# The order of VectorE, ScalarE, GpSimd and the transfers: from the framework's scheduler to a list schedule written in the kernel

## The chip, the cores and the metric

The kernel runs on one core of one Trainium2 chip. A core has five engines with a queue of instructions each: TensorE (PE, matmuls; PEld are its weight loads), VectorE (DVE), ScalarE (ACT), GpSimd (POOL) and SyncE (SP), which here only issues transfers. The metric is the device time of one execution in microseconds (us), the median of several runs. One more execution is taken with a profiler; its "span" runs from the first to the last instruction.

## The reference

A block over x of 2048 tokens by 512 features, all in float32. The weights are scaled so that sums are large, and the kernel computes each product of two float32 matrices from halves in float16.

```python
xn = layernorm(x)
# A: sliding-window attention, 32 heads of 16, window 256
q, k, v = split(xn @ wqkv)
p = softmax(where(mask, q @ k.T * 16**-0.5, -1e9))
s = (p @ v) @ wo
# B: gated feed-forward, 512 -> 1792 -> 512
h = silu(xn @ w1) * (xn @ w3)
g = silu(h @ w2)
out = x + s * g
```

## The kernel before

**Tiling.** The tokens go in NT = 4 passes t of 512; within a pass the attention goes by NG = 4 groups of 8 heads and two halves p, so there are 32 attention "units" (t, g, p). The feed-forward goes by 14 blocks f of 128 columns of w1, w3 and rows of w2. Every float32 operand is split into a high float16 part and the rest, and a product is three matmuls (high x high, high x low, low x high).

**A unit.** `pass1` (L588 to L606) forms scores for the row maxima: four times a matmul into a PSUM bank pair `s` or `po`, then a masked maximum on DVE (L600, accumulated into M). The maxima are scaled (L605, L606), turned by a small matmul (L615), copied (L621) and sent through DRAM into two extra rows of the query tile `qa` (L623, L625). Two units later `pass2` forms the scores the other way round with the maxima subtracted (L662), adds the mask on DVE (L669), takes the exponent on ACT (L672) and multiplies by the values (L690). `finish` copies the sums out of PSUM (ACT L700, DVE L703) and sends them on; `normalise` inverts the denominators (L727), has them spread by DMA, multiplies on POOL and splits the result (ACT L740, POOL L300).

**Dense work.** `project` makes queries and keys (PE L534, ACT L543, DVE L547, then to DRAM and back), `value` the values (PE L504, ACT L507). `gate_up` makes one block f (PE L856, 24 matmuls): a tanh on ACT (L867), two products on DVE (L871, L876), a split on ACT and POOL (L880, L300). `down` multiplies by w2 and accumulates over four groups of blocks (PE L901; ACT L914 or DVE L917). `total` multiplies by wo and forms the output (PE L943; DVE L938, L947).

**Weights.** In pass 0 every block of w1, w3, w2 is loaded as float32, its squares are summed (ACT L231 and L814, or DVE L233) to choose a power of two as its scale, and it is scaled and split (ACT L303, L304, POOL L300); the split halves are stored to DRAM and loaded back in passes 1 to 3. So pass 0 has much more ACT, POOL and transfer work than the others. The layernorm of pass t + 2 is prepared in pass t (L406 to L424: statistics, an inverse square root by Newton steps on tiles of 128 x 4, centring), and then turned by matmuls (L462, L471, L472).

**Memory.** Two PSUM banks `m` take turns for the dense products, two bank pairs `s` and one pair `po` serve the attention. 39 slots in SBUF (`fpool`) are handed out by hand (`take`, `give`) for weights and intermediate results.

**What sets the order.** The program is traced by a planner of its own (`spread`, `run`, `later`, `more`), which interleaves pieces of dense work between batches of attention. TensorE runs in exactly the order traced:

```python
ORDERED = {ENGINE.PE}
with _tile.TileContext(nc) as tc, tc.manual_schedule(engines=ORDERED):
    tile_block(tc, *args)
```

The four other queues are ordered by the framework's scheduler, which starts from the order traced; `urgent()` moves an instruction forward by a priority of 200. In the first part of the program eight ties by hand (`tc.issue_after`, with the dictionary `lasts` of instructions) put chosen instructions behind others on their engine. Semaphores follow from the data and the final order.

## Time and profile before

| | |
|---|---|
| median of 3 runs | 840.1 us (838.94 to 843.25) |
| profiled execution, span | 835.6 us |
| the median beside that span | 4.5 us longer |
| PE busy | 809.6 us, 97% |
| DVE, ACT, POOL busy | 614.4, 408.2, 196.7 us |
| HBM traffic over the span | 125 GB/s |

Matmuls overlap in the records, so that a full row of matmuls reads as busy throughout, and PE's idle time is the time in which none was under way. A wait in a row of the timeline stands in brackets behind the instruction that waited: how long its engine had been idle, and whose end let it go. Idle time of the four other engines costs nothing unless PE, or the end, waits for them.

### The profile page before, as it was taken

To read this page: it belongs to the slowest core of one execution; us is meant where nothing else is said; L and a number is where in the kernel's file an instruction comes from. 1 tells how busy PE (TensorE), PEld (TensorE's weight loads), DVE (VectorE), ACT (ScalarE), POOL (GpSimd) and SP (SyncE) were. 2 spreads that over 40 slices of the span, in tenths; PEclk is the share of its full clock that TensorE was granted. 3 is DMA by queue.
4 is the path that set the end of the run, shared out by engine and by line. 5 is a ranking of instruction groups with operands and counts; after the bars stand their busy time and mean duration, and the time that the engine had idled before them with its cause. 6 is when DMAs were issued, how large, how long until landed. Compare 5 with 4: busy or idle time off the path is not lost.

```text
span 835.6 us, 22584 instructions
## 1 busy us (share of the span) xinstructions
PE 809.6 (97%) x8750; PEld 381.5 (46%) x8750; DVE 614.4 (74%) x2034; ACT 408.2 (49%) x598; POOL 196.7 (24%) x325
## 2 busy tenths in 40 slices
PE   9999898899999999999999999999999999999998
PEld 4434344434444444444445444444444444444444
DVE  8788767966797767798778876687777777676435
ACT  6799776373436444344433444443444443443521
POOL 2236264051313203111110211121111104031211
PEclk9999999999999999999999999999999999999999
DMA  9977556146633453453442535533443443434101
GB/s 281 260 232 237 165 181 184 47 152 199 189 96 95 110 140 108 138 155 110 130 121 72 140 94 154 142 111 102 119 143 88 112 117 107 116 96 125 55 21 52
DMA packets 95323, 110.62 MB, mean 132 GB/s; under 512 B 17200, under 2 KB 60528, under 8 KB 95216
## 3 DMA queue, kind: packets, MB, share of 16 engines
q1 hardware_dynamic: 94928, 108.67, 44.9%
q8 instruction: 68, 1.11, 0.6%
q10 hardware_dynamic: 288, 0.52, 0.2%
q14 instruction: 39, 0.32, 0.1%
HBM read 76.28 MB, written 28.57 MB: 125 GB/s over the span
## 4 chain that ended last, share of the span: by engine, by line
PE 68%; DVE 9%; issue 7%; DMA 6%; ACT 5%; POOL 3%; SPq 2%; POOLq 0%; ACTq 0%; DVEq 0%
PE m L856 24%; PE m L901 13%; PE po L690 8%; PE m L534 6%; PE s L662 5%; PE m L943 4%; PE m L504 3%; POOL slot L300 3%; DVE junk L600 2%; PE s L588 2%; DMA slot<-in_B_w_dram 2%; DMA qa<-dQ 1%; DVE s L669 1%; PE po L588 1%; ACT slot L303 1%
## 5 line engine op out<-in xcount | busy, mean ns | idle before, releaser
L300 POOL TENSOR_TENSOR slot<-slot,slot 128x256 f16<-128x256 f32 (+1 forms) x228 | 148.3, 677 | 575.7 <-ACT slot L880 464.5
L856 PE MATMUL m<-XH,slot 128*128 128x512 f16 x896 | 267.3, 380 | 4.3 <-DVE slot L547 2.5
L672 ACT ACTIVATE pt<-s,es 128x1024 f32<-128x1024 f32 x152 | 167.7, 1113 | 180.5 <-DVE s L669 177.3
L856 PEld LDWEIGHTS <-slot 128*128 128x128 f16 x1344 | 124.8, 98 | 159.9 <-issue 17.7
L856 PE MATMUL m<-XL,slot 128*128 128x512 f16 x448 | 169.8, 379 | 0.0
L901 PE MATMUL m<-slot,slot 128*128 128x512 f16 x672 | 158.1, 383 | 2.2 <-DVE slot L917 1.0
L669 DVE TENSOR_TENSOR s<-s,MK 128x256 f32<-128x256 f32 (+2 forms) x280 | 118.6, 435 | 49.2 <-PE s L662 48.2
L600 DVE CUSTOM_DVE_ANT_0 junk<-s,MW 128x320 bf16<-128x320 f32 x276 | 134.3, 486 | 24.7 <-PE s L588 15.7
L901 PEld LDWEIGHTS <-slot 128*128 128x128 f16 x672 | 62.5, 98 | 82.2 <-issue 12.3
L600 DVE CUSTOM_DVE_ANT_0 junk<-po,MW 128x320 bf16<-128x320 f32 x172 | 83.7, 487 | 5.6 <-DVE al L272 0.4
L690 PE MATMUL po<-pt,V 64*32 64x320 f32 (+4 forms) x2880 | 77.7, 343 | 0.5 <-DVE pp L277 0.5
L880 ACT CAST slot<-slot 128x512 f16<-128x512 f32 x56 | 34.5, 616 | 67.4 <-DVE slot L876 67.1
L690 PEld LDWEIGHTS po<-pt,V 64*32 64x32 f32 x2880 | 51.9, 106 | 24.1 <-PE s L588 4.7
L662 PE MATMUL s<-qa,KA 50*64 50x320 f16 (+3 forms) x1472 | 58.0, 259 | 1.4 <-DVE M L600 0.6
L871 DVE SCALAR_TENSOR_TENSOR slot<-slot,m 128x512 f32<-128x512 f32 x56 | 38.3, 684 | 28.0 <-ACT slot L867 27.0
L662 PEld LDWEIGHTS <-KA 50*64 50x64 f16 x1472 | 30.2, 105 | 55.7 <-issue 36.1
L867 ACT ACTIVATE slot<-m,sgs 128x512 f32<-128x512 f32 x56 | 38.4, 685 | 27.8 <-PE m L856 27.6
L588 PE MATMUL s<-KA,qa 48*64 48x320 f16 (+2 forms) x648 | 45.3, 294 | 6.7 <-DVE M L600 4.0
L917 DVE SCALAR_TENSOR_TENSOR slot<-m,dsc,slot 128x512 f32<-128x512 f32 x48 | 35.9, 747 | 15.9 <-PE m L901 15.6
L876 DVE SCALAR_TENSOR_TENSOR slot<-m,slot 128x512 f32<-128x512 f32 x56 | 38.5, 688 | 12.3 <-PE m L856 11.4
L534 PE MATMUL m<-XH,whi 128*128 128x512 f16 x120 | 44.7, 381 | 1.4 <-DVE slot L876 0.9
L534 PE MATMUL m<-XL,whi 128*128 128x512 f16 x120 | 44.5, 379 | 0.0
(152 smaller groups left out, 870.7 us busy)
## 6 DMA issues: line engine op xcount, KB each, us to landing
slot<-dW SPq DMA_DIRECT2D x126, 256.0 KB
slot<-in_B_w_dram SPq DMA_DIRECT2D x42, 256.0 KB
dW<-slot SPq DMA_DIRECT2D x42, 256.0 KB
slot<-in_A_x_dram SPq DMA_DIRECT2D x30, 256.0 KB
KA<-dK SPq DMA_DIRECT2D x24, 288.0 KB
qa<-dQ SPq DMA_DIRECT2D x32, 192.0 KB
dQ<-slot SPq DMA_DIRECT2D x16, 256.0 KB
dK<-slot SPq DMA_DIRECT2D x16, 256.0 KB
```

The costliest lines, as they stand in the source:

```text
L300: op(out[:, c], a[:, c], b[:, c])
L534: nc.tensor.matmul(cell["pp"], a[:, k, c, :], b[:, c, :], start=(c, i) == parts[0][0], stop=(c, i) == parts[-1][-1])
L588: nc.tensor.matmul(s[64 * c:64 * c + 64, r, :n], qa[rows, 2 * p + a, ii * P + 64 * c:ii * P + 64 * c + 64], ka[rows, 2 * p + a, e - n:e], ...
L600: nc.vector.tensor_tensor_reduce(out=junk[:, :n], in0=s[:, r, :n], in1=mask, scale=1.0, scalar=NEG, op0=ALU.add, op1=ALU.max, accum_out=M[ ...
L662: nc.tensor.matmul(s[64 * h:64 * h + 64, r, o:o + 64 * n], ka[rows, 2 * p + a, 64 * (m + 4):64 * (m + 5)], qa[rows, 2 * p + a, 64 * (m + k ...
L669: nc.vector.tensor_add(v, v, MK[:, kind, of:of + n, :].unsqueeze(1).to_broadcast([P, 2 * len(which), n, 64]))
L672: nc.scalar.activation(pt, s, AF.Exp, scale=es)
L690: nc.tensor.matmul(cell["po"][32 * i:32 * i + 32, h, 64 * (m + k):64 * (m + k + n)], V[64 * h:64 * h + 64, (4 * t + m // 2) % VB, hd * VW: ...
L856: nc.tensor.matmul(cell[k], w[:, (a * NC + c) * P:(a * NC + c + 1) * P], b[:, c, :], start=c == 0 and i == 0, stop=c == NC - 1 and i == 2)
L867: nc.scalar.activation(sg, cell[0], AF.Tanh, scale=sg_scale[:, f:f + 1])
L876: nc.vector.scalar_tensor_tensor(sg, cell[1], 0.5 * HS / (WS * XS)**2, sg, op0=ALU.mult, op1=ALU.mult)
L901: nc.tensor.matmul(ps, hh[:, a * TW + b * P:a * TW + (b + 1) * P], w[:, c * D:(c + 1) * D], start=f == f0 and i == 0, stop=f == f1 - 1 and ...
```

## The change

The eight ties, the dictionary `lasts` and its assignments go. A function `listed(tc)` is called once the whole program has been traced. It works on the list of all instructions, before the framework schedules them:

- `arrange` finds which instruction depends on which, by the regions that they read and write, by the reuse of tiles and by their PSUM banks. It gives every instruction a price: for PE by columns, type and tile size, plus 160 ns where the tile size changes; for ACT 130 + 0.98 n, for DVE 80 + 1.05 n, for POOL 40 + 2.6 n ns, n being the elements per partition; 420 ns for the issue of a transfer, with a latency and a time by its bytes.
- `deadlines` takes PE's order with PE never waiting ("nominal") and goes back from it: the latest start of each other instruction that keeps PE in time.
- `listed` then simulates all five queues. PE goes in its own order. Each other engine takes, of what is ready, the instruction with the earliest deadline; it stays idle for a while if something more urgent is about to be ready. An instruction counts as ready somewhat later than its inputs are (up to 1 us, 4 us behind a transfer) where its deadline leaves 2 us. Transfers with a distant deadline stand back while over 1.5 us of transfers are under way. After the first, each of three rounds uses the round before to see what is coming; the shortest is kept.
- The order found is fixed: every instruction of DVE, ACT, POOL and SP is chained to the one before it on its queue. No semaphore belongs to such a link.

What PE does and in which order, the tiles, slots and transfers stay as they are.

```diff
     def split(hi, lo, raw, s):
-        lasts["hi"] = nc.scalar.activation(hi, raw, AF.Copy, scale=s)
-        lasts["cut"] = nc.vector.scalar_tensor_tensor(lo, raw, s, hi, op0=ALU.mult, op1=ALU.subtract)
+        nc.scalar.activation(hi, raw, AF.Copy, scale=s)
+        nc.vector.scalar_tensor_tensor(lo, raw, s, hi, op0=ALU.mult, op1=ALU.subtract)
...
-    with tc.issue_after(lasts["centre"].ins):
-        qk[0][3]((1,))
+    qk[0][3]((1,))
...
-    with tc.issue_after(lasts["hi"].ins), tc.issue_after(lasts["x"].ins):
-        qk[1][1]()
+    qk[1][1]()
...
+def arrange(tc):
...
+    def cost(i):
+        n = 1
+        for s, c in i.outs[0].ap[1:]:
+            n *= c
+        if i.engine == ENGINE.PE:
+            t = i.tile_size
+            return n * (4 if i.ins[0].dtype == F32 else 1) / 2.4 * t[0] * t[1] / P**2 + 2
+        kind = type(i).__name__
+        if kind == "InstDMACopy":
+            return 420
...
+        if i.engine == ENGINE.Activation:
+            return 130 + 0.98 * n + 50 * (len(i.outs) > 1)
+        if i.engine == ENGINE.DVE:
+            return 80 + 1.05 * n + (6 * n if kind == "InstReciprocal" else 0) + 45 * (len(i.outs) > 1)
+        return 40 + 2.6 * n
...
+    extra = [1350 + carry(i) if d else 130 if i.engine != ENGINE.PE else 180 for i, d in zip(made, dma)]
...
+            if i.engine != ENGINE.PE:
+                latest[k] = min([latest[a] - (extra[k] if made[a].engine != i.engine or dma[k] else 0)
+                                 for a in after[k]] + [end]) - took[k]
...
+def listed(tc):
...
+            if k is None:
+                can = sorted((k for k in waiting[e] if ready[k] <= s), key=lambda k: latest[k])
+                k = can[0]
+                if ready_then:
...
+                    for k in can:
+                        if all(latest[j] >= latest[k] or ready_then[j] >= s + took[k] or latest[j] + SLACK >= s + took[k]
+                               for j in coming):
+                            break
+                    else:
+                        t = min(j_t for j_t in (ready_then[j] for j in coming))
+                        free[e] = max(t, s + 1)
+                        continue
+                if dma[k] and pipe > s + BACK and latest[k] > s + NEAR:
+                    free[e] = min([pipe - BACK] + [ready[j] for j in waiting[e] if ready[j] > s])
+                    continue
...
+            for a in after[k]:
+                wanted[a] -= 1
+                when = done + (60 if dma[k] else extra[k] if made[a].engine != e else 0)
+                margin = AFTER_DMA if dma[k] else AFTER if made[a].engine != e else 0
+                ready[a] = max(ready[a], when, min(when + margin, latest[a] - CLOSE))
...
+        if best_end is None or max(start) < best_end:
+            best_end, best_order = max(start), order
+    for e in engines[1:]:
+        for a, b in zip(best_order[e], best_order[e][1:]):
+            tc.add_manual_dep(made[b], made[a].name,
+                              mybir.DependencyInfo(mybir.DependencyClass.NoSync, mybir.DependencyReason.DATA), reason="order")
...
+ROUNDS, SHIFT = 3, False
+SLACK, BACK, NEAR = 300, 1500, 5000
+AFTER_DMA, AFTER, CLOSE = 4000, 1000, 2000
...
     with _tile.TileContext(nc) as tc, tc.manual_schedule(engines=ORDERED):
         tile_block(tc, *args)
+        listed(tc)
```

## The prediction

> **What bounds the kernel now.** I read the page first, then stages, then what TensorE waits for, then the timeline around single waits. The page's busy times:

> ```profile
> span 835.6 us, 22584 instructions
> PE 809.6 (97%) x8750; PEld 381.5 (46%) x8750; DVE 614.4 (74%) x2034; ACT 408.2 (49%) x598; POOL 196.7 (24%) x325
> ```

> TensorE (PE) sets the time, and the change leaves its order and its work alone. So only its idle time can be won: 835.6 - 809.6 = 26.0 us. The table of stages (start:end, length, then busy time of PE, PEld, DVE, ACT, POOL; granted clock; DMA share; GB/s) says where that lies:

> ```profile
> 0.00:40.00 40.00, 37.41 (x198) 16.73 (x199) 30.68 (x116) 29.56 (x58) 10.42 (x41) 1.00 1.00 266
> 40.00:120.00 80.00, 72.61 (x649) 32.58 (x648) 64.00 (x257) 67.66 (x133) 35.82 (x56) 0.98 0.64 207
> 120.00:240.00 120.00, 110.84 (x1336) 54.37 (x1339) 90.05 (x343) 62.28 (x99) 40.21 (x63) 1.00 0.50 152
> 240.00:800.00 560.00, 557.02 (x6391) 262.68 (x6391) 413.52 (x1295) 242.50 (x299) 105.01 (x158) 1.00 0.40 114
> 800.00:836.00 36.00, 31.74 (x201) 15.12 (x180) 16.18 (x26) 6.22 (x10) 5.26 (x8) 1.00 0.14 42
> ```

> PE's idle time is 2.59 us to 40 us, 7.39 us from 40 to 120, 9.16 us from 120 to 240, only 2.98 us in the 560 us that follow, and 4.26 us at the end (0.4 of it past the span). 40 to 240 us is the stretch that holds 16.55 us, and there no other engine is full: DVE 154 of 200 us, ACT 130. The engines have the time; the question is in what order they spend it. The longest waits of PE by name:

> ```profile
> PE s L588 <- DVE M L600: 4.0, 2, 2.9
> PE m L856 <- DVE slot L547: 2.5, 3, 1.3
> PE po L588 <- DVE XL L472: 1.9, 2, 1.1
> ```

> All three end with a DVE instruction that frees a PSUM bank or fills an operand. The costliest single one, at 88 us, with an undisturbed run of 12 equal matmuls (501.49) for comparison:

> ```profile
> 88.38 0.41 PE L662 MATMUL s<-qa,KA 50*64 50x320 f16 x10
> 91.71 0.25 PE L588 MATMUL s<-KA,qa 48*64 48x128 f16 x4 [2.92 <-DVE M L600]
> 91.89 4.45 PE L901 MATMUL m<-slot,slot 128*128 128x512 f16 x12
> ...
> 501.49 2.76 PE L901 MATMUL m<-slot,slot 128*128 128x512 f16 x12
> ```

> PE stands 2.92 us, and then 12 matmuls take 4.45 instead of 2.76 us: 1.69 us more, the only stage with a granted clock under 1.00. What DVE did meanwhile, with one row of POOL:

> ```profile
> 83.89 0.69 DVE L414 TENSOR_SCALAR r<-ve 128x4 int32<-128x4 int32 x1
> ...
> 86.70 0.16 DVE L418 TENSOR_TENSOR sq<-r 128x4 f32<-128x4 f32 x1
> 86.77 2.55 POOL L300 TENSOR_TENSOR slot<-slot,slot 128x256 f16<-128x256 f32 x4 [0.33 <-POOL slot L300]
> ...
> 88.12 0.59 DVE L418 TENSOR_TENSOR sq<-r 128x4 f32<-128x4 f32 x1
> ...
> 89.57 0.17 DVE L421 TENSOR_SCALAR rs<-r 128x4 f32<-128x4 f32 x1
> ...
> 90.30 0.48 DVE L600 CUSTOM_DVE_ANT_0 junk<-s,MW 128x320 bf16<-128x320 f32 x1
> ```

> It worked on the layernorm of the next 512 tokens (rstd, L411 to L421), wanted much later, while the maxima that PE's bank waits for (L600) stood behind. The same instruction, L418, takes 0.16 us where POOL pauses (0.33 us up to 86.77) and 0.59 us while POOL runs. Two more, with another pattern: DVE idle behind ACT, which does other things first.

> ```profile
> 120.15 0.61 ACT L304 CAST slot<-slot 128x512 f16<-128x512 f32 x1
> 120.66 0.69 ACT L867 ACTIVATE slot<-m,sgs 128x512 f32<-128x512 f32 x1
> ...
> 121.38 0.69 DVE L871 SCALAR_TENSOR_TENSOR slot<-slot,m 128x512 f32<-128x512 f32 x1 [2.72 <-ACT slot L867]
> ...
> 143.72 0.63 ACT L814 ACTIVATE sqa<-slot 128x512 bf16<-128x512 f32 x1
> 144.25 0.19 ACT L814 ACTIVATION_READ_ACCUMULATOR sqa<-slot 128x1 f32 x1
> 144.34 0.57 ACT L700 COPY os<-po 128x512 f32<-128x512 f32 x1
> ...
> 144.94 0.62 DVE L703 TENSOR_TENSOR os<-os,po 128x448 f32<-128x448 f32 x1 [2.48 <-ACT os L700]
> ```

> Weight splits (L304) and weight squares (L814) are done ahead of a tanh (L867) and a copy (L700) for which DVE, and behind DVE PE, wait. Over the span the table of waits has these pairs, and SP's own longest:

> ```profile
> DVE slot L871 <- ACT slot L867: 27.0, 24, 2.7
> DVE os L703 <- ACT os L700: 27.5, 23, 4.6
> SPq L709 <- DVE os L703: 108.1, 28, 14.3
> ```

> So the stalls I looked at are of order, not of work. That is what the change touches.

> **The change, part by part.** No instruction is added or removed on any engine, and no transfer; what changes is the order on DVE, ACT, POOL and SP, and all of it is fixed in advance by a plan made with prices (`cost`) and PE's order.

> *The hand ties* (eight, all before the second attention unit, so in the first stage). They kept weight squares behind splits and projections. Their loss is covered if the plan puts the splits by their deadline, as it is made to. If not, a split waits for a pair of squares:

> ```profile
> L231 ACT ACTIVATE sqa<-slot 128x512 bf16<-128x512 f32 x34 | 21.3, 627 | 1.8 <-DMA slot<-in_A_wqkv_dram 1.3
> L231 ACT ACTIVATION_READ_ACCUMULATOR sqa<-slot 128x1 f32 x34 | 6.4, 189 | 0.0
> ```

> 2 x (0.63 + 0.19) = 1.6 us. Gain at most the 2.59 us of that stage less 1.05 us before the first matmul: 1.5 us. I take 0, keeping -1.5 to +1.6.

> *DVE, ACT and POOL from 40 to 240 us.* At stake are 16.55 us of idle time and 1.69 us of slow clock, 18.24 us. An order by PE's deadlines puts L600 before the rstd chain, L867 before L304, L700 before L814. Bounds: nothing recovered, or all. I take three quarters, 13.7 us, since the three stalls above are all of the kind that the deadline decides, and a plan with fixed prices will miss some. POOL has 76 of 200 us of work here and feeds weights that are needed later; its order has slack.

> *The same from 240 to 800 us.* 2.98 us can be won; I take half, 1.5 us. Here is also the largest risk: an order that stands almost without stalls is replaced. What it may cost depends on the plan's prices, and one of them is far off. It prices a matmul of L690 at n x 4 / 2.4 x 64 x 32 / 16384 + 2 ns:

> ```profile
> L690 PE MATMUL po<-pt,V 64*32 64x320 f32 x1024 | 48.7, 431 | 0.5 <-DVE pp L277 0.5
> L690 PE MATMUL po<-pt,V 64*32 64x192 f32 x512 | 21.8, 323 | 0.0
> L690 PE MATMUL po<-pt,V 64*32 64x128 f32 x448 | 19.9, 274 | 0.0
> L690 PE MATMUL po<-pt,V 64*32 64x64 f32 x512 | 16.7, 217 | 0.0
> L690 PE MATMUL po<-pt,V 64*32 64x256 f32 x384 | 15.9, 388 | 0.0
> L690 PE MATMUL po<-pt,V 64*32 64x320 f32 (+4 forms) x2880 | 77.7, 343 | 0.5 <-DVE pp L277 0.5
> ```

> That is 68.7, 42.0, 28.7, 15.3 and 55.3 ns for these forms, 133.7 us in all against 77.7 us measured; over 32 attention units 4.18 against 2.43 us each. The plan believes PE 1.75 us later behind each of these bursts than it is. A bank that is drained 1.75 us late costs PE nothing as long as the other bank lasts: 2.76 us for 12 matmuls, less the draining instruction:

> ```profile
> L876 DVE SCALAR_TENSOR_TENSOR slot<-m,slot 128x512 f32<-128x512 f32 x56 | 38.5, 688 | 12.3 <-PE m L856 11.4
> L419 DVE SCALAR_TENSOR_TENSOR sq<-sq,ve 128x4 f32<-128x4 f32 x12 | 3.7, 309 | 0.4
> ```

> 2.76 - 0.69 = 2.07 us, just above 1.75. So I take a loss of 2 us over the stretch; bounds 0 and 1.75 us for each of its 24 bursts (2344 of the 2880 matmuls are counted there, at 96 a unit), 42 us.

> *SP's queue.* All transfers but two of the first loads are issued by SP, and they are reordered too, past waits like L709's, of up to 14.3 us. Weights of the later passes are asked for two blocks of F ahead (24 + 12 matmuls each at 2.76 us a dozen, so over 16 us ahead), which covers one such wait; without that cover the longest would be a stall of 14.3 us. I take 0; the DMA share of 0.40 leaves room.

> *The end.* Stage five is PE's own work and the last sum and store; 0.

> Sum, on the profiled execution: 835.6 - 13.7 - 1.5 + 2.0 = 822.4 us of span. The median of the runs, 840.1 us, is 4.5 us above that span; 822.4 + 4.5 = 826.9. Forecast **827 us**, its own range 819 to 835.

> [...]

> **The rivals.**

> *A, all order.* The plan removes every stall and costs nothing: 835.6 - 18.24 - 2.98 - 1.5 + 4.5 = 817 us. For it: idle engines in every stage. Against: prices are fixed and durations aren't.

> *B, the early stalls come back elsewhere.* The plan prices an instruction like L419 at 80 + 1.05 x 4 = 84 ns; the row above has 309 on average. The twelve from L414 (83.89) to the end of L421 (89.74) took 5.9 us where the plan counts 12 x 84 ns, 1.0 us. A plan that thinks it fits the chain in before L600 is ready makes the very stall of 88 us again. ACT is also 85% busy from 40 to 120 us. A quarter is then recovered, 4.6 us, against the 2 us lost: 835.6 - 4.6 + 2.0 + 4.5 = 837.5 us, no change that a measurement can tell. Against: the plan works in single instructions, so L600 can step in between two of the chain. [...]

> *C, slower: the plan's late TensorE.* At each burst of L690, DVE takes something else in the 1.75 us by which the plan thinks PE late, and the drain comes after the other bank has run out. It decides from the point where DVE already stands over 0.3 us behind (2.07 - 1.75). Half of the 1.75 us lost at 24 bursts is 21 us; with half of the early gain, 9.1 us: 835.6 - 9.1 + 21 + 4.5 = 852 us. For it: DVE is 74% busy there (413.5 of 560 us), and the stretch has almost nothing to win. Against: the error is the same everywhere and deadlines decide by comparison; nine bursts that lose all 1.75 us (15.7 us) only cancel the gain.

> *D, the plan does nothing.* If its edges gave the order that was there, the time would be 840. The stalls shown are against its rule, so I give it little and count it with B.

> **How the numbers follow.** Forecast 0.53, A 0.11, B with D 0.17, C 0.19. 0.5% (4.2 us), about what a measurement of this kernel can tell, puts the borders at 835.9 and 844.3 us. Faster: forecast, A and a small part of B, 0.67. Same: the rest of B, 0.14. Slower: C, 0.19. The range runs from 815 us, below A, to 848 us, where the milder half of C is in; it leaves out the heavier C and little below A.

> **What would show it.** Right: PE's idle time from 40 to 240 us falls from 16.55 to about 5 us; no stage has a clock under 1.00; L871's wait for L867 and L703's for L700 shrink; L600 stands among the rstd chain; 240 to 800 us stays within some 4 us of idle. B: another wait of 2 us or more on L600 behind L411 to L421. C: waits of PE on DVE (L871, L876, L917) right behind L690 bursts, and idle time spread evenly over 240 to 800 us. Wrong altogether: a stall on a weight load or on a KA or qa transfer, that is, SP's queue.

## The result and the profile after

The changed kernel takes 832.8 us (median of 5 runs, 832.03 to 833.4), the kernel before 838.9 us beside it (median of 5, 837.18 to 843.25): a ratio of 0.9923, with a 95% interval of 0.99 to 0.9947. That is 5.8 us above the forecast of 827, inside its range and its likeliest case's own range, and faster by more than 0.5%. The gain, though, is 6.1 us where 13.1 (840.1 to 827) were forecast. Lines behind the removed `lasts = {}` carry numbers one lower in this kernel: L599 here is L600 before, L870 is L871, L702 is L703, and the rstd chain is L410 to L420.

The profile after, its head and busy times:

```profile
span 830.5 us, 22573 instructions
PE 808.1 (97%) x8750; PEld 381.9 (46%) x8750; DVE 636.6 (77%) x2034; ACT 409.2 (49%) x598; POOL 200.5 (24%) x325
```

Its table of stages, in the columns of the prediction:

```profile
0.00:40.00 40.00, 35.81 (x200) 16.79 (x201) 32.41 (x120) 29.68 (x57) 9.04 (x39) 1.00 1.01 278
40.00:120.00 80.00, 74.36 (x665) 33.53 (x664) 66.49 (x259) 66.77 (x129) 35.56 (x54) 0.96 0.67 194
120.00:240.00 120.00, 114.25 (x1390) 56.31 (x1388) 102.31 (x350) 66.45 (x105) 43.42 (x66) 0.99 0.53 159
240.00:800.00 560.00, 557.05 (x6369) 262.54 (x6368) 420.53 (x1283) 240.62 (x300) 107.14 (x160) 1.00 0.40 113
800.00:836.00 36.00, 26.60 (x134) 12.70 (x132) 14.90 (x24) 5.65 (x9) 5.32 (x8) 0.96 0.13 42
```

PE's idle time by stage went from 2.59 to 4.19 us, 7.39 to 5.64, 9.16 to 5.75, 2.98 to 2.95, and stayed at 3.9 at the end: 26.0 to 22.4 us in all. What grew is the time at half clock. The granted clock of 0.96 in the second stage and 0.99 in the third comes from two stretches of 6.83 and 3.41 us at half speed, 10.24 us together; before there was one of 3.41. The two now, in the same columns:

```profile
109.89:116.72 6.83, 5.49 (x17) 2.05 (x18) 6.45 (x29) 2.24 (x3) 0.73 (x2) 0.50 0.07 14
171.33:174.74 3.41, 3.03 (x8) 1.07 (x8) 3.16 (x15) 2.31 (x4) 0.12 (x1) 0.50 0.21 79
```

The first starts 1.34 us before a stall ends, the second 0.38 us before one ends. By estimate half of the rest is lost, (10.24 - 1.34 - 0.38) / 2 = 4.3 us now, 1.7 before. What PE waits for, by name:

```profile
PE m L855 <- DVE slot L870: 4.7, 2, 4.0
PE s L587 <- DVE NM L604: 4.0, 1, 4.0
```

Most of the waits of 1 to 3 us are gone, and two of 4.0 us stand in their place. The pairs of DVE and ACT that the prediction named have shrunk in their sums, from 27.0 and 27.5 us:

```profile
DVE slot L870 <- ACT slot L866: 21.5, 21, 2.6
DVE os L702 <- ACT os L699: 9.6, 14, 2.0
```

The timeline around these two stalls:

```profile
105.13 0.17 DVE L413 TENSOR_SCALAR r<-ve 128x4 int32<-128x4 int32 x1
...
106.13 0.16 DVE L417 TENSOR_TENSOR sq<-r 128x4 f32<-128x4 f32 x1
106.29 2.57 POOL L300 TENSOR_TENSOR slot<-slot,slot 128x256 f16<-128x256 f32 x4 [1.92 <-DMA KA<-dK]
...
107.65 0.61 DVE L417 TENSOR_TENSOR sq<-r 128x4 f32<-128x4 f32 x1
...
109.12 0.17 DVE L420 TENSOR_SCALAR rs<-r 128x4 f32<-128x4 f32 x1
...
109.79 0.48 DVE L599 CUSTOM_DVE_ANT_0 junk<-s,MW 128x320 bf16<-128x320 f32 x1
...
111.23 0.32 PE L587 MATMUL s<-KA,qa 48*64 48x128 f16 x4 [4.03 <-DVE NM L604]
...
166.47 0.52 DVE L413 TENSOR_SCALAR r<-ve 128x4 int32<-128x4 int32 x1
...
170.24 0.17 DVE L420 TENSOR_SCALAR rs<-r 128x4 f32<-128x4 f32 x1
...
170.98 0.68 DVE L870 SCALAR_TENSOR_TENSOR slot<-slot,m 128x512 f32<-128x512 f32 x1
...
171.71 1.01 PE L855 MATMUL m<-XH,slot 128*128 128x512 f16 x2 [3.97 <-DVE slot L870]
```

Both times DVE does the twelve small instructions of the rstd chain (L413 to L420) in one piece, in 4.2 us (105.13 to 109.29) and 3.9 us (166.47 to 170.41), while what PE waits for (L599 and behind it L604, L870) stands behind it. The first is the very chain that the prediction showed at 88 us, moved and still in the way. The second is that of the next block of tokens, which DVE did before at 150 to 156 us with 22 other instructions in between. And again L417 takes 0.16 us ahead of POOL's work (106.13) and 0.61 us during it (107.65).

One more count matters. PE runs the same 8750 matmuls in the same order in both kernels, so their start times can be compared one by one. The matmul that started at 40.0 us before starts 0.3 us earlier now, the one of 240.0 us 5.7 us earlier, the one of 800.1 us 5.1 us earlier, and the end comes 5.1 us earlier (835.6 - 830.5). So the first stage won 0.3 us, although PE is busy for 1.6 us less in it, 40 to 240 us won 5.4, and 240 to 800 us lost 0.5. Idle time alone doesn't tell this. PE's busy time fell by 1.5 us (809.6 to 808.1) with the same matmuls, though by the estimate above the clock added 4.3 - 1.7 = 2.6 us to it. What the remainder, 4.1 us, comes from is not shown.

### The profile page after: what moved, and what is told of

Same layout as the page of the kernel before. It is cut to its first block, busy times and chain, and to the rows that moved or that the text cites. A ratio compares the mean times of both kernels' runs of the same rounds, so it can differ in the third digit from the quotient of the medians.

```text
span 830.5 us, 22573 instructions
## 1 busy us (share of the span) xinstructions
PE 808.1 (97%) x8750; PEld 381.9 (46%) x8750; DVE 636.6 (77%) x2034; ACT 409.2 (49%) x598; POOL 200.5 (24%) x325
## 4 chain that ended last, share of the span: by engine, by line
PE 79%; DVE 14%; DMA 2%; issue 2%; SPq 1%; ACT 1%; POOL 1%; DVEq 0%; ACTq 0%; POOLq 0%
PE m L855 30%; PE m L900 16%; PE po L689 8%; PE m L533 7%; PE s L661 5%; PE m L942 4%; PE m L503 4%; DVE junk L599 3%; PE s L587 3%; DVE s L668 2%; PE po L587 1%; DVE st L405 1%; DVE slot L870 1%; DMA qa<-dQ 1%; POOL slot L300 1%
## 5 line engine op out<-in xcount | busy, mean ns | idle before, releaser
L671 ACT ACTIVATE pt<-s,es 128x1024 f32<-128x1024 f32 x152 | 168.9, 1114 | 220.6 <-DVE s L668 196.7
L855 PE MATMUL m<-XH,slot 128*128 128x512 f16 x896 | 270.3, 384 | 5.5 <-DVE slot L870 4.7
L300 POOL TENSOR_TENSOR slot<-slot,slot 128x256 f16<-128x256 f32 (+1 forms) x228 | 150.5, 685 | 508.5 <-ACT slot L879 382.9
L668 DVE TENSOR_TENSOR s<-s,MK 128x256 f32<-128x256 f32 (+2 forms) x280 | 121.8, 437 | 72.9 <-PE s L661 68.0
L900 PE MATMUL m<-slot,slot 128*128 128x512 f16 x672 | 155.9, 380 | 0.7 <-DVE slot L546 0.3
L599 DVE CUSTOM_DVE_ANT_0 junk<-s,MW 128x320 bf16<-128x320 f32 x276 | 134.5, 487 | 23.4 <-PE s L587 14.6
L599 DVE CUSTOM_DVE_ANT_0 junk<-po,MW 128x320 bf16<-128x320 f32 x172 | 84.0, 489 | 11.0 <-DVE M L599 0.5
L689 PE MATMUL po<-pt,V 64*32 64x320 f32 (+4 forms) x2880 | 77.7, 343 | 0.0
L699 ACT COPY os<-po 128x512 f32<-128x512 f32 x32 | 18.7, 583 | 78.4 <-PE po L689 71.5
L870 DVE SCALAR_TENSOR_TENSOR slot<-slot,m 128x512 f32<-128x512 f32 x56 | 38.1, 681 | 22.2 <-ACT slot L866 21.5
L879 ACT CAST slot<-slot 128x512 f16<-128x512 f32 x56 | 34.3, 613 | 27.6 <-DVE slot L875 27.5
```

What stands on the lines that cost most here:

```text
L300: op(out[:, c], a[:, c], b[:, c])
L599: nc.vector.tensor_tensor_reduce(out=junk[:, :n], in0=s[:, r, :n], in1=mask, scale=1.0, scalar=NEG, op0=ALU.add, op1=ALU.max, accum_out=M[ ...
L668: nc.vector.tensor_add(v, v, MK[:, kind, of:of + n, :].unsqueeze(1).to_broadcast([P, 2 * len(which), n, 64]))
L671: nc.scalar.activation(pt, s, AF.Exp, scale=es)
L689: nc.tensor.matmul(cell["po"][32 * i:32 * i + 32, h, 64 * (m + k):64 * (m + k + n)], V[64 * h:64 * h + 64, (4 * t + m // 2) % VB, hd * VW: ...
L855: nc.tensor.matmul(cell[k], w[:, (a * NC + c) * P:(a * NC + c + 1) * P], b[:, c, :], start=c == 0 and i == 0, stop=c == NC - 1 and i == 2)
```

## The experiments

The theory: the two stalls and their half clock are what kept the gain small, and their cause is the price of small DVE instructions (84 ns in `cost`), by which the plan sees a chain of 1.0 us and fits it in whole. Its rivals: the price of L690 (the prediction's C), the order on another engine, the margins (`AFTER`, `AFTER_DMA`), and the lost ties. Each edit below is against the changed kernel. The ratios are to the kernel before, run beside it (medians 840.55 us for e1 to e4, 839.62 for e5 to e8, 839.68 for e9 to e12).

To change prices at all, a flaw of the plan had to go. `box` in `arrange` works out which region of a tile an instruction touches. For the flattened maxima, "p r a i -> p (r a i)", it carries an overflow one dimension outward and no further, so the plan doesn't see that L604 reads what L599 writes for r = 1. With other prices it put L604 ahead of L599, an order that can't be run. This correction is in all kernels but e3 and e5. It was not timed alone, but with the prices of the changed kernel it gives the same order on every queue as without it, so by itself it changes nothing.

```diff
             if high[d] > dims[d]:
+                more = (high[d] - 1) // dims[d]
                 low[d:], high[d:] = [0] * (len(dims) - d), dims[d:]
                 if d:
-                    high[d - 1] = dims[d - 1]
+                    high[d - 1] += more
```

**e1: small DVE instructions at 200 ns.** 200 ns is about what they take where POOL rests: 0.16 us and a pause of 0.04 (in the changed kernel L419 starts at 105.93 and L417 at 106.13 us).

```diff
-            return 80 + 1.05 * n + (6 * n if kind == "InstReciprocal" else 0) + 45 * (len(i.outs) > 1)
+            return max(200, 80 + 1.05 * n) + 0 * (n <= 16) + (6 * n if kind == "InstReciprocal" else 0) + 45 * (len(i.outs) > 1)
```

> The kernel after, with two edits in its plan alone: every VectorE instruction is priced at 200 ns at least (before, 84 ns for a tile of 128 x 4), and the region of a flattened tile is found in full, since without that the plan puts L604 ahead of a maximum that it reads and the program can't be ordered. My theory: the two new stalls of 4.03 and 3.97 us, and the 10.2 us at half clock that go with them, come from the rstd chain (L410 to L420), twelve dependent instructions that the plan counts as 1.0 us and that took 4.2 to 4.6 us. With 200 ns the plan opens the chain for the maxima, no wait of TensorE is over 2 us, and the time falls from 832.8 to 820 to 826 us. Rival: VectorE is full from 80 to 200 us, and the same 8 us of waits come back under other names: 830 to 835 us.

Measured: 814.74 us (814.16 to 816.88), ratio 0.9693 [0.9675, 0.9711]. Its head and busy times:

```profile
span 812.8 us, 22579 instructions
PE 802.2 (99%) x8750; PEld 380.3 (47%) x8750; DVE 630.2 (78%) x2034; ACT 409.1 (50%) x598; POOL 198.9 (24%) x325
```

Its second to fourth stages:

```profile
40.00:120.00 80.00, 79.86 (x754) 36.81 (x756) 71.24 (x284) 73.70 (x138) 40.58 (x62) 1.00 0.71 210
120.00:240.00 120.00, 118.71 (x1474) 58.71 (x1471) 105.64 (x382) 67.02 (x102) 40.67 (x63) 1.00 0.57 161
240.00:800.00 560.00, 559.15 (x6304) 263.36 (x6290) 415.35 (x1245) 237.23 (x299) 109.31 (x164) 1.00 0.40 110
```

From 40 to 240 us 1.4 us of idle time are left of 16.55, and the clock is full in all three. The timeline of the chain:

```profile
97.62 0.16 DVE L413 TENSOR_SCALAR r<-ve 128x4 int32<-128x4 int32 x1
...
98.83 0.48 DVE L599 CUSTOM_DVE_ANT_0 junk<-s,MW 128x320 bf16<-128x320 f32 x1
...
102.11 0.16 DVE L417 TENSOR_TENSOR sq<-r 128x4 f32<-128x4 f32 x1
102.18 0.68 DVE L870 SCALAR_TENSOR_TENSOR slot<-slot,m 128x512 f32<-128x512 f32 x1
102.78 0.49 DVE L599 CUSTOM_DVE_ANT_0 junk<-s,MW 128x320 bf16<-128x320 f32 x1
...
104.28 0.15 DVE L418 SCALAR_TENSOR_TENSOR sq<-sq,ve 128x4 f32<-128x4 f32 x1
```

The maxima (L599) and the drain L870 now stand among the chain's instructions. One price and the region are all that differs from the changed kernel, and 18 us are gained (832.8 to 814.7), more than expected. The chain also misses POOL's work here (99.36 to 100.66 and 105.70 to 108.28 us), and its instructions in these rows take 0.15 or 0.16 us; how much of the 18 us comes from that is not shown.

**e2: the same, and 400 ns more for up to 16 elements**, the 0.6 us of an instruction beside POOL's work (0.59 to 0.66 us in the four that start from 106.32 to 108.29 us in the changed kernel).

```diff
+            return max(200, 80 + 1.05 * n) + 400 * (n <= 16) + (6 * n if kind == "InstReciprocal" else 0) + 45 * (len(i.outs) > 1)
```

> As e1_small200, with a price of 600 ns for VectorE instructions of up to 16 elements per partition, what they take while GpSimd runs. My theory: this is the price that matters at the two stalls; the chain is opened further, and the time is 819 to 826 us, equal to e1 or up to 2 us better. Rival: a price that is wrong on the other side for most small instructions (0.16 us when GpSimd pauses) makes the plan idle or late elsewhere: 3 us or more above e1. If VectorE is full: 830 to 835 us.

Measured: 866.4 us, ratio 1.0298 [1.0282, 1.0313]: much slower. What PE waits for, by name:

```profile
PE po L587 <- DVE os L702: 11.1, 2, 7.5
```

The timeline of the longest (SPq is SP's queue of transfers):

```profile
262.91 2.47 SPq L708 DMA_DIRECT2D on<-os  x4
...
266.85 0.59 ACT L699 COPY os<-po 128x512 f32<-128x512 f32 x1 [2.20 <-DMA on<-os]
267.46 0.62 DVE L702 TENSOR_TENSOR os<-os,po 128x448 f32<-128x448 f32 x1 [3.70 <-ACT os L699]
268.14 0.48 PE L587 MATMUL po<-KA,qa 48*64 48x320 f16 x4 [7.45 <-DVE os L702]
```

None of its longest stalls is behind the chain. Here DVE itself idles 3.70 us, for a copy (L699) that waited until a transfer (L708) had read the tile `os`; that transfer had waited for ACT and POOL in its turn (1.2 and 1.4 us). The mean granted clock is 0.976 over a span of 865.1 us, so about 41 us (2 x 0.024 x 865.1) ran at half. A price near what these instructions take beside POOL made the plan worse as a whole. Why the other engines' orders suffer is only argued: a plan that thinks DVE over-full gives everything behind it late start times.

**e3: no plan.** Ties gone, `listed` not called.

```diff
-        listed(tc)
```

> The kernel after without the call of listed: the hand ties are gone and no plan takes their place; the framework's scheduler orders VectorE, ScalarE, GpSimd and SyncE alone. My theory: the ties are worth little, 0 to 1.6 us, so 838 to 841 us, and the gain is the plan's. Rival: the ties held the first 40 us together, and without them the time is 845 us or more; then the plan's own worth is larger than the 6 us measured.

Measured: 841.17 us, ratio 1.0005 [0.9986, 1.0024]. Its first stage:

```profile
0.00:40.00 40.00, 35.22 (x191) 15.66 (x192) 29.37 (x112) 29.20 (x58) 8.40 (x38) 1.00 0.96 258
```

PE has done 191 matmuls there against 198 with the ties, and the matmul that started at 40.0 us starts at 41.7. So the ties hold about 1.7 us of the first stage (one execution of each), and the whole doesn't show it: the kernel before has spans from 834.1 to 841.2 us in the executions beside e1 to e12. The whole gain of the change is then the plan's.

**e4: L690's price lowered to what was measured** (77.7 / 133.7 of it). These matmuls take float32 as it is, without halves.

```diff
-            return n * (4 if i.ins[0].dtype == F32 else 1) / 2.4 * t[0] * t[1] / P**2 + 2
+            return n * ((2.3 if t[1] == 32 else 4) if i.ins[0].dtype == F32 else 1) / 2.4 * t[0] * t[1] / P**2 + 2
```

> The kernel after (with the region edit of e1), with one other price: the matmuls of L690 at 2.3 instead of 4 passes per float32 column, which brings them from 133.7 us in sum near the 77.7 us measured. My theory: the error cost nothing, since TensorE's idle time from 240 to 800 us stayed at 2.95 us: 831 to 835 us, with the two 4 us stalls still there or moved by the new order. Rival: the late TensorE in the plan costs in every unit, though under what reads as idle: 825 us or less.

Measured: 831.15 us, ratio 0.9884 [0.987, 0.9899], 1.6 us under the changed kernel. Its fourth stage:

```profile
240.00:800.00 560.00, 556.83 (x6369) 262.56 (x6368) 420.53 (x1285) 240.79 (x300) 106.46 (x160) 1.00 0.42 113
```

And its longest waits of PE:

```profile
PE m L533 <- DVE slot L546: 4.1, 1, 4.1
PE s L587 <- DVE NM L604: 3.3, 1, 3.3
```

The fourth stage is as it was (557.05), and two long stalls remain, both behind the rstd chain again: DVE does eleven of its instructions in a row from 105.62 to 109.02 us and ten from 168.67 to 173.11 us, ahead of L604 and L546. That price costs nothing that can be seen.

**e5: the chain shortened** from twelve instructions to six, with the prices of the changed kernel. It leaves out two of the three Newton steps of the layernorm's rstd.

```diff
-            for i in range(3):
+            for i in range(1):
```

> The kernel after with its own prices, but two of the three Newton steps of the layernorm's inverse square root (L417 to L419) left out: that part of the computation is missing. The chain from L410 to L420 has 6 instructions in place of 12, and in the passes where the stalls lie it stands in the plan's order at the same place, in one piece. My theory: the chain itself is what TensorE waits for, so the stalls of 4.03 and 3.97 us shrink by what the six took (2 to 3 us each), to under 2.1 us, and the half clock behind them goes: 832.8 less about 5 and less about 5, so 821 to 825 us. Rival: the chain only fills time in which the maxima were not ready (VectorE full, or L870 late because of ScalarE): both waits stay above 3 us, and 831 to 834 us.

Measured: 823.97 us, ratio 0.982 [0.9798, 0.9842]. Its second and third stages:

```profile
40.00:120.00 80.00, 76.75 (x705) 35.12 (x704) 65.44 (x266) 69.70 (x133) 38.25 (x59) 1.00 0.67 194
120.00:240.00 120.00, 114.92 (x1393) 56.76 (x1392) 105.09 (x357) 64.98 (x102) 39.59 (x61) 1.00 0.56 165
```

And the longest wait of PE:

```profile
PE m L855 <- DVE slot L870: 2.5, 2, 2.2
```

The chain stands in one piece at nearly the same places and takes 1.2 us (104.62 to 105.79) and 2.1 us (162.39 to 164.49) in place of 4.2 and 3.9. The long stall on L870 shrinks from 4.0 to 2.2 us, that on L604 is gone, and the clock stays at 1.00. Half of the chain's instructions are worth 8.8 us: the chain is the cause, and the half clock behind it (4.3 us by the estimate above) is a good part of the price. (The plan is made anew for the shorter chain, so some other lines move too.)

**e6, e7, e8: e1's plan, given to some engines only**; the others keep the order that the framework gives them.

```diff
-    for e in engines[1:]:
+    for e in [ENGINE.DVE]:
```

(e7: DVE and ACT; e8: POOL and SP.)

> The plan of e1_small200 (814.7 us), with the order fixed for VectorE alone; ScalarE, GpSimd and SyncE are left to the framework's scheduler. My theory: some stalls need ScalarE's order as well (a tanh or a copy that stands behind weight splits), so about half of e1's gain: 825 to 832 us. Rival 1: VectorE's order is all that counts: 814 to 819 us. Rival 2: an order on one engine made for another order on the others hurts: over 840 us.

> The plan of e1_small200 with the order fixed for VectorE and ScalarE; GpSimd and SyncE are left to the framework's scheduler. My theory: these two hold the stalls, so nearly all of e1's gain: 814 to 820 us. Rival: SyncE's queue carries a good part, since transfers of low urgency stand before urgent ones in the old order: 825 us or more.

> The plan of e1_small200 with the order fixed for SyncE and GpSimd alone; VectorE and ScalarE are left to the framework's scheduler. My theory: no gain, since TensorE's waits of before end with VectorE or ScalarE: 837 to 842 us. Rival: the transfers' order carries a good part: 832 us or less.

Measured: 846.43 us, 1.0089 [1.0061, 1.0117]; 824.09 us, 0.9823 [0.9794, 0.9851]; 846.1 us, 1.0084 [1.0057, 1.0111]. With DVE alone planned, PE now waits for ACT, in e6's table of waits:

```profile
PE s L587 <- ACT pt L671: 4.6, 3, 3.4
```

With ACT planned too, one large stall is left, in e7's table of waits:

```profile
PE m L503 <- ACT V L506: 8.6, 1, 8.6
```

The timeline of ACT there:

```profile
41.33 0.63 ACT L813 ACTIVATE sqa<-slot 128x512 bf16<-128x512 f32 x1 [11.55 <-DMA slot<-in_B_w_dram]
41.96 0.67 ACT L506 ACTIVATE V<-m,uv 128x512 f32<-128x512 f32 x1
```

ACT stood 11.55 us before the squares of a weight (L813), for a load (L804) that SP brings late in its own order: the first such load is issued at 35.35 us, in e1 at 20.12. The copy that PE waits for (L506) is fixed behind it. DVE's order alone, and POOL's and SP's, make the kernel slower than before. DVE with ACT makes it faster, but stays 9.4 us short of e1, nearly all by this one stall: the matmul of 40.0 us starts 8.6 us later than in e1, and from there e7 falls back by 1.1 us more. The orders belong together.

**e9: the floor at 300 ns.**

```diff
+            return max(300, 80 + 1.05 * n) + 0 * (n <= 16) + (6 * n if kind == "InstReciprocal" else 0) + 45 * (len(i.outs) > 1)
```

> The plan of e1_small200 with a price of 300 ns at least for VectorE instructions, the mean that L419 has (309 ns) where e1 takes the 200 ns of an undisturbed one. My theory: between e1 (814.7 us) and e2 (600 ns, 866.4 us) the plan becomes worse as soon as its VectorE is fuller than the real one, and 300 ns is a little too much: 815 to 825 us. Rival: the mean is the right price, and the time falls under e1, to 811 to 814 us.

Measured: 823.17 us, ratio 0.9803 [0.9788, 0.9817]. So the mean (309 ns) is not the better price. Waits of another kind are back, on POOL's splits of weights (L300: 3.9 us in four, the longest 1.5) and on a query transfer at the start (`qa`, 1.6 us). They are shorter than the stalls of the changed kernel, yet the last section shows two of them that were followed by half clock.

**e10: e1 without margins.**

```diff
-AFTER_DMA, AFTER, CLOSE = 4000, 1000, 2000
+AFTER_DMA, AFTER, CLOSE = 0, 0, 2000
```

> The plan of e1_small200 without its margins (an instruction counts as ready when its inputs are; AFTER and AFTER_DMA 0). My theory: the margins are what lets a fixed order stand real durations; without them in-order queues stand behind late transfers more often: 818 to 826 us. Rival: prices decide, margins don't: within 2 us of e1, 813 to 817 us.

Measured: 831.91 us, ratio 0.9901 [0.9885, 0.9918]: 17 us worse than e1, with waits like these:

```profile
PE s L587 <- DMA qa<-dQ: 2.6, 2, 1.8
PE m L900 <- POOL slot L300: 2.6, 2, 2.4
```

They are behind DMA and POOL alike, which fits a plan that counts on each input the moment it should be ready, and so pays for every duration that is longer than its price. That last step is argued: no row compares the plan's times with the trace's.

**e11: e1 and e4's price of L690 together.** The edits are those two.

> e1_small200 together with the price of L690 from e4_pe_price. e4 came out at 831.2 us with the old small price, 1.7 us under the kernel after. My theory: with the long chain out of the way there is next to nothing left for TensorE to win from 240 to 800 us (0.85 us of idle time in e1), so within 1.5 us of e1: 813 to 816 us. Rival: the true pace of TensorE gives better deadlines at the start too: under 812 us.

Measured: 819.77 us, ratio 0.9763 [0.9749, 0.9778]: 5 us worse than e1, by the start:

```profile
0.00:40.00 40.00, 33.42 (x161) 15.00 (x162) 28.53 (x103) 28.61 (x60) 6.79 (x35) 0.96 1.03 283
```

PE is busy 33.42 us there and the clock is 0.96; e1 has 35.33 and 1.00. The matmul of 40.0 us starts 3.6 us later than in e1, behind a wait of 2.8 us for a query transfer (`qa`). A price nearer to the trace gave a worse order.

**e12: e1, with the eight ties given to the plan as edges.**

```diff
+    for ins, lo, hi in TIES:
+        for one in ins:
+            for k, i in enumerate(made):
+                if lo <= spot[i.name] < hi and i.engine == one.engine:
+                    before[k].add(number[one.name])
```

> e1_small200 with the eight hand ties of the kernel before given to the plan as edges between instructions of one engine. In the first 40 us TensorE idles 4.67 us in e1 and 2.59 us in the kernel before. My theory: the ties are worth these 2 us once the rest is in order: 812 to 814 us. Rival: the start is bound by the arrival of the weights, and the ties only move the wait: 814 to 816 us, or more where they hold back something urgent.

Measured: 820.76 us, ratio 0.9781 [0.9763, 0.9799]. First and third stage:

```profile
0.00:40.00 40.00, 36.48 (x197) 16.70 (x198) 31.69 (x117) 29.12 (x57) 8.08 (x37) 1.00 1.03 290
120.00:240.00 120.00, 116.14 (x1418) 56.98 (x1411) 106.04 (x370) 64.92 (x100) 39.29 (x60) 1.00 0.54 160
```

PE is busy 1.15 us more in the first stage than in e1 (36.48 against 35.33), but it has done only one matmul more by then, and the matmul of 40.0 us starts 0.3 us earlier; the ties are worth no more than that here. The third stage loses 2.57 us (116.14 against 118.71), where no tie reaches. So e9, e11 and e12, all close to e1, lie at 820 to 823 us. Some 5 to 8 of the 18 us that e1 gains on the changed kernel seem to be one fortunate order, and the other 10 to 13 come with the price.

## Why the prediction was right, and where not

- *Only idle time can be won, 26.0 us.* The limit was too low where it mattered: compared matmul by matmul, e1 wins 20.4 us from 40 to 240 us, where 18.24 were counted as all there was, and 1.4 us of idle time are still left. The time that PE is busy fell as well, by 7.4 us in e1 (809.6 to 802.2, 1.7 of it the clock). It is no fixed amount in these traces: the same 8750 matmuls read as 809.6 and as 802.2 us.
- *Three quarters of 18.24 us from 40 to 240 us.* This is the step that failed: 5.4 us by the count of matmuls, not 13.7. Small stalls did go; but 8.0 of the 11.39 us of idle time that are left are two stalls behind the rstd chain, and the half clock took some 2.6 us more than before. The prediction's own rival B had the mechanism and the numbers (84 ns against 309, a chain of 1.0 us in the plan and 5.9 in the trace). It was given a chance of its own, as if the chain either stood in the way or didn't; the plan removed many small stalls, moved the chain's stall from 88 to 107 us and made another behind the next block's chain at 167. Its sign of being right, L600 among the chain's instructions, did not show; rival B's sign, another wait behind the chain, did. Its argument against, that the plan works in single instructions, falls: at the two stalls nothing stepped in between. e1 and e5 show it from both sides: by the count of matmuls this stretch wins 20.4 us with the price raised and 11.6 with the chain shortened.
- *240 to 800 us, 1.5 won and 2 lost.* The net, a loss of 0.5 us, came out as measured by the count of matmuls, but neither of its two terms shows: idle time stayed as it was, 2.98 to 2.95 us, so this agreement is luck. C's price error was real and harmless (e4), as its counter-argument said: it is the same everywhere. That half of the idle time could be won there is seen in e1 (3.0 us won by the count of matmuls, 0.85 us of idle time left).
- *Ties 0, within -1.5 to +1.6.* Right for the whole (e3: 1.0005) and for their own stage in the changed kernel, which won 0.3 us. Without a plan that stage loses about 1.7 us (e3), at the bound.
- *SP's queue 0.* Nothing speaks against it in the changed kernel: the longest wait of PE on a `qa` transfer is 0.7 us. That SP's order needs no plan doesn't follow: e7 pays 8.6 us where SP and POOL keep their own.
- *The end 0.* Right, 3.9 and 3.9 us.
- *4.5 us from span to median.* It was 2.3 us (832.8 - 830.5). The profiled execution of before was one of the shorter ones: the kernel's new median lies 3.3 us above its span, while within one execution of the changed kernel the two differ by 1.9 us (832.4 and 830.5).
- *The sum.* Against a span of 822.4 us the trace has 830.5: 8.1 us more. By the count of matmuls 40 to 240 us fell 8.3 us short, the first stage was 0.3 better, and the fourth and the end were as forecast. The 8.1 us, less 2.2 of the offset, are the 5.9 us by which the median lies above 826.9. So two errors of opposite sign met, and the larger one is more than half of the forecast gain: that the time came out inside the likeliest case's range owes something to luck.
- *The rivals.* A (817, a span of 812.9) is not what the change does, but e1 reaches it, with a span of 812.8 and a median of 814.7; the two medians differ by the offset alone. B is half true, C and D are false: D by the stalls that went and by e3.

## What to carry to other kernels

A list schedule is as good as its prices where a chain of tiny instructions meets a deadline: price them by what they take in the trace, with their pauses, and then time a few neighbouring prices, since 200, 300 and 600 ns gave 815, 823 and 866 us. The orders of all engines belong to one plan, with a margin on every edge between engines; DVE's order alone was slower than no plan. To see where a change gains, compare the start times of the same matmuls; idle time in fixed windows misread the first stage here. In a prediction, a mechanism that has been seen in the trace and that the plan's prices can't avoid belongs into the sum as a partial loss, not beside it as a rival.

## What the runs showed of the hardware

Half clock came after shorter and broken waits too. Two windows of e9 around 82 us:

```profile
78.70:82.10 3.40, 1.63 (x22) 0.56 (x21) 3.37 (x10) 3.34 (x6) 2.26 (x4) 1.00 0.77 227
82.10:85.90 3.80, 3.24 (x8) 0.91 (x8) 3.49 (x14) 2.52 (x5) 3.80 (x7) 0.55 0.77 234
```

And the matmuls behind PE's two waits in its timeline:

```profile
80.18 0.59 PE L900 MATMUL m<-slot,slot 128*128 128x512 f16 x2 [1.38 <-POOL slot L300]
82.62 4.63 PE L900 MATMUL m<-slot,slot 128*128 128x512 f16 x13 [0.91 <-POOL slot L300]
```

Two waits of 1.38 and 0.91 us, with some 1.5 us of matmuls between them, and the clock falls to 0.55 in the next window; thirteen matmuls take 4.63 us. By the window's mean clock 2 x 0.45 x 3.80 = 3.4 us of it ran at half. But e5's single wait of 2.19 us, behind L870 and up to 166.03 us, was followed by none: its mean clock is 1.000 over the span.

The 1.69 us that the prediction counts for the slow matmuls behind the stall at 88 us is about half of one stretch of 3.41 us. The stall at 107 us was followed by 6.83 us of half clock, of which 1.34 were idle anyway; it cost (6.83 - 1.34) / 2 = 2.7 us by the same estimate.
